# An attention kernel's VectorE exponentials: three shifted bit patterns with 64-bit adds on GpSimd, and PSUM banks and SBUF slots in shared pools

## Chip, core and metric

The kernel runs on one core of a Trainium2 chip. TensorE multiplies matrices into PSUM, ScalarE computes functions, VectorE does elementwise work, GpSimd works on SBUF, SyncE issues DMAs. The engines run at the same time (ScalarE, VectorE and TensorE are busy for 98, 94 and 92% of the same span in the kernel before), each in the fixed order that the program gives it, and wait for each other (TensorE's matmuls for ScalarE 36.6 us there). The metric is the time of one execution in microseconds (us), median of several runs; smaller is better.

## The reference, cut to what matters

There are two attention blocks of the same size, joined at the end. Block A is linear attention and is small. Block B is full softmax attention with 32 heads of width 16 over 2048 positions, and it makes nearly all the work:

```python
q, k, v = qkv[0], qkv[1], qkv[2]          # each [1, 32, 2048, 16]
scores = jnp.einsum("bhqd,bhkd->bhqk", q, k) * Dh ** -0.5
p = _softmax(scores, axis=-1)
o = jnp.einsum("bhqk,bhkd->bhqd", p, v)
```

The scores hold 32 x 2048 x 2048 numbers. In tiles of 128 partitions by 512 columns ("blocks") that is 2048 blocks of exponentials. A runtime test decides whether the plain exponential without subtracting the maximum is safe; with these inputs it always is, so the general path behind it never runs.

## The kernel before: the parts that the change touches

The source lays the instructions out in advance: a small scheduler written in Python assumes a duration for each operation, decides what goes to which engine in which order, and emits the fixed program. Each of the 2048 blocks goes through a score matmul (QK) into a PSUM bank, an exponential on ScalarE *or* on VectorE, and a weighted-sum matmul (PV) that accumulates into one PSUM bank. A unit is 64 blocks that share one PV bank. A round is four PV matmuls. Where TensorE would have nothing to do, the scheduler puts in filler matmuls with zero weights (`ZW`), which add nothing to the result.

ScalarE takes three or two banks at once (`ABL`), with two fixed slots. VectorE has two banks of its own, `DB`, which it shares with the projections and block A:

```python
    ABL = (3, 2)
    ...
        SCR = [ps("pS%d" % i, [128, ABL[i] * 512], F32) for i in range(2)]
        PVb = ps("pPV", [128, 512], F32)
        DB = ps("pD", [128, 1024], F32)
    ...
                    sch.add("act", lambda e: e.activation(PT[:, row, c0:c0 + w], SCR[sl][:, 0:w], ACTF.Exp, scale=SC),
                            reads=skeys(sl), writes=[("PT", row, sl)])
```

On VectorE the kernel builds the exponential out of other operations. It scales and shifts the score, writes it as a 16-bit integer and reads those bits as float16 (the exponent field then holds the integer part of the power of two). Three more VectorE operations split and correct the pattern, and two matmuls per block add the two parts:

```python
                    sch.add("dve", lambda e: e.tensor_scalar(DI[:, buf, i * 512:(i + n) * 512], DB[:, b0 * 512:(b0 + n) * 512],
                                                             ESC, EB, op0=ALU.mult, op1=ALU.add), ...
            ops = [
                (0.06 + w * 0.00026, lambda e: e.tensor_scalar(Q, I, 0x3FF, 0x3800, op0=ALU.bitwise_and, op1=ALU.bitwise_or), ik, qk_),
                (0.08 + w * 0.00052, lambda e: e.tensor_tensor(Qh, Ih, Qh, op=ALU.mult), ik + qk_, qk_),
                (0.06 + w * 0.00026, lambda e: e.tensor_scalar(I, I, 0xFC00, 8, op0=ALU.bitwise_and, op1=ALU.bitwise_or), ik, ik)]
```

GpSimd only sets up constants. The first of them, an identity matrix, is needed at once: TensorE transposes the first pieces of x with it.

```python
        def mk_ident(t, key):
            sch.add("pool", lambda e: e.memset(t[:], 0.0), writes=[key])
            sch.add("pool", lambda e: e.affine_select(out=t[:], in_=t[:], compare_op=ALU.not_equal, fill=1.0,
                                                     base=0, pattern=[[-1, 128]], channel_multiplier=1),
                   reads=[key], writes=[key])
```

## Time and profile before

| before | value | where it is read |
|---|---|---|
| time | 760.04 us | median of 3 runs, 759.95 to 761.25 |
| span in the profile | 758.5 us | the page's head; 1.6 us of the time lie outside it |
| ScalarE / VectorE / TensorE / GpSimd busy | 98 / 94 / 92 / 1% | part 1 |
| first exponential starts | 8.59 us | timeline of ScalarE |
| blocks on ScalarE / VectorE | 1592 / 456 | counts of the groups |

Parts 1 and 4 of the page of the kernel before: busy us, share of the span and number of instructions by engine; then the chain of waits that ended last, by engine.

```profile
PE 695.9 (92%) x6229; PEld 234.4 (31%) x6229; DVE 716.1 (94%) x1235; ACT 739.8 (98%) x675; POOL 8.5 (1%) x27
...
ACT 94%; PE 4%; DVE 1%; DMA 1%; SPq 0%; issue 0%; ACTq 0%
```

ScalarE (ACT) is busy nearly all the time and carries 94% of the chain, so only a change that shortens ScalarE's own work, or its idle time, can shorten the kernel. VectorE (DVE) is nearly full too, which matters for what can be moved to it.

The groups of the page: source line, engine, operation, output<-input, shapes, count | busy us, mean ns of one | idle us just before them and who ended most of it.

```profile
L869 ACT ACTIVATE PT<-pS 128x1536 f16<-128x1536 f32 x637 | 732.5, 1482 | 5.1 <-PE pD L712 2.8
L811 DVE TENSOR_SCALAR DI<-pD 128x512 int16<-128x512 f32 (+1 forms) x442 | 304.0, 698 | 18.1 <-PE pD L712 15.9
L925 DVE TENSOR_TENSOR DQ<-DI,DQ 128x1536 f16<-128x1536 f16 x153 | 144.1, 942 | 1.6
L924 DVE TENSOR_SCALAR DQ<-DI 128x1536 int16<-128x1536 int16 x153 | 83.7, 547 | 1.1
L926 DVE TENSOR_SCALAR DI<-DI 128x1536 int16<-128x1536 int16 x153 | 83.2, 544 | 0.7
```

The exponentials wait only 5.1 us in all. The last three lines are the chain behind VectorE's conversions: 311 us, as much as the conversions themselves.

The mean of 1482 ns for an exponential can't be used as its cost, since the records of neighbours overlap: 637 times 1482 ns would be 944 us, in a span of 758.5. The longest pieces of the chain of waits give the cost, because within one there is no idle time (start us, us, what):

```profile
342.91 61.02 ACT PT L869 x54
```

54 alternating three-bank and two-bank exponentials in 61.02 us make 2.26 us a pair. Where exponentials follow each other without a gap in this trace, their ends lie 1.343 us (three banks), 0.917 us (two) and 0.490 us (block A's, one bank) apart, in the median. The differences of these are 0.426 and 0.427 us per 512 columns, which leaves 0.063 us for each instruction, and 1.343 and 0.917 make the 2.26 of a pair; I call this the cost law. For the 318, 319 and 32 smaller ones of block A (0.49 us each) it gives 735.1 us (to within 0.2, by rounding); ScalarE's busy time without its 3.7 us of other work is 736.1.

### The profile page before, as it was taken

What the parts mean: (1) busy time and instruction counts of PE and PEld (TensorE: products, weight loads), DVE (VectorE), ACT (ScalarE), POOL (GpSimd) and SP (SyncE); (2) the same over time, 40 slices, a digit from 0 to 9 for tenths busy, and PEclk for the clock granted to TensorE, in tenths of its full rate; (3) what the DMA queues carried; (4) which work ended last, traced back from release to release, by engine and by line L of the source; (5) the groups of instructions that cost most, each with busy time, mean ns of one, the idle gap of its engine ahead of it and who ended that gap; (6) DMA issues with size and microseconds to landing.
All of it is one profiled execution on the core that took longest, in us unless ns stands there. A gap on an engine that the chain in (4) does not pass through costs nothing.

```text
span 758.5 us, 14741 instructions
## 1 busy us (share of the span) xinstructions
PE 695.9 (92%) x6229; PEld 234.4 (31%) x6229; DVE 716.1 (94%) x1235; ACT 739.8 (98%) x675; POOL 8.5 (1%) x27
## 2 busy tenths in 40 slices
PE   8999999999999899999989899999899889999996
PEld 4333232333333323223222332222242232323232
DVE  6899999899999989989999999989999999999994
ACT  6999999999999999999999999999999999999995
POOL 4000000000000000000000000000000000000000
PEclk9999999999999989999999999999999999999999
DMA  9900000000000000000000000000002001110001
GB/s 197 247 2 1 1 1 9 10 12 1 1 2 1 1 1 2 14 9 15 22 22 1 1 22 22 22 9 15 15 2 42 1 2 50 29 35 8 15 15 32
DMA packets 36568, 17.27 MB, mean 23 GB/s; under 512 B 27536, under 2 KB 35984, under 8 KB 36496
## 3 DMA queue, kind: packets, MB, share of 16 engines
q1 hardware_dynamic: 35408, 15.61, 8.6%
q8 instruction: 51, 0.84, 0.5%
q10 hardware_dynamic: 1088, 0.66, 0.3%
q14 instruction: 21, 0.17, 0.1%
HBM read 4.46 MB, written 4.19 MB: 11 GB/s over the span
## 4 chain that ended last, share of the span: by engine, by line
ACT 94%; PE 4%; DVE 1%; DMA 1%; SPq 0%; issue 0%; ACTq 0%
ACT PT L869 91%; ACT EA L571 2%; PE pPV L996 1%; PE pS L712 1%; DMA Wb<-in_B_wqkv_dram 1%; PE pS L1048 0%; PE pD L462 0%; DVE DI L811 0%; DVE DQ L925 0%; SPq L333 0%; ACT KNa L444 0%; DVE KNa L444 0%; PE pPV L1209 0%; PE pS L1090 0%; PE pD L661 0%
## 5 line engine op out<-in xcount | busy, mean ns | idle before, releaser
L869 ACT ACTIVATE PT<-pS 128x1536 f16<-128x1536 f32 x637 | 732.5, 1482 | 5.1 <-PE pD L712 2.8
L811 DVE TENSOR_SCALAR DI<-pD 128x512 int16<-128x512 f32 (+1 forms) x442 | 304.0, 698 | 18.1 <-PE pD L712 15.9
L712 PE MATMUL pS<-QT,KM 32*128 32x512 bf16 x1592 | 248.4, 386 | 50.0 <-ACT PT L869 36.6
L996 PE MATMUL pPV<-PT,VV 128*17 128x512 f16 x1592 | 204.7, 384 | 1.2 <-DVE OT L1023 1.2
L712 PE MATMUL pD<-QT,KM 32*128 32x512 bf16 x456 | 169.2, 386 | 0.8 <-issue 0.5
L925 DVE TENSOR_TENSOR DQ<-DI,DQ 128x1536 f16<-128x1536 f16 x153 | 144.1, 942 | 1.6
L712 PEld LDWEIGHTS pS<-QT,KM 32*128 32x128 bf16 x1592 | 60.8, 91 | 273.1 <-ACT PT L869 262.1
L996 PE MATMUL pPV<-DQ,VV 128*17 128x512 f16 x456 | 102.7, 386 | 1.0 <-DVE OT L1023 0.8
L996 PE MATMUL pPV<-DI,VV 128*17 128x512 f16 x456 | 101.7, 383 | 0.0
L1209 PE MATMUL pPV<-xTb,ZW 128*17 128x256 bf16 x593 | 93.9, 274 | 0.0
L924 DVE TENSOR_SCALAR DQ<-DI 128x1536 int16<-128x1536 int16 x153 | 83.7, 547 | 1.1
L926 DVE TENSOR_SCALAR DI<-DI 128x1536 int16<-128x1536 int16 x153 | 83.2, 544 | 0.7
L996 PEld LDWEIGHTS pPV<-PT,VV 128*17 128x17 bf16 x1592 | 43.9, 88 | 73.2 <-issue 63.1
L1209 PEld LDWEIGHTS pPV<-xTb,ZW 128*17 128x17 bf16 x593 | 45.2, 91 | 39.4 <-issue 29.4
L712 PEld LDWEIGHTS pD<-QT,KM 32*128 32x128 bf16 x456 | 40.1, 91 | 14.6 <-DVE DI L811 6.9
L580 PE MATMUL pD<-Wa,xTa 128*128 128x256 bf16 x256 | 39.0, 277 | 0.0
L462 PE MATMUL pD<-xTb,Wb 128*128 128x512 bf16 x120 | 34.7, 383 | 1.0 <-DVE DI L811 0.6
L996 PEld LDWEIGHTS pPV<-DQ,VV 128*17 128x17 bf16 x456 | 23.0, 88 | 24.7 <-issue 16.8
L996 PEld LDWEIGHTS pPV<-DI,VV 128*17 128x17 bf16 x456 | 26.5, 90 | 9.6 <-DVE DI L926 1.0
L571 ACT ACTIVATE EA<-pD 128x512 bf16<-128x512 f32 x32 | 27.3, 854 | 0.0
L1023 DVE STREAM_TRANSPOSE OT<-pPV 128x512 f32<-128x512 f32 x32 | 22.6, 708 | 4.4 <-PE pPV L996 4.4
L580 PEld LDWEIGHTS pD<-Wa,xTa 128*128 128x128 bf16 x256 | 20.2, 98 | 16.8 <-issue 9.0
(92 smaller groups left out, 327.6 us busy)
## 6 DMA issues: line engine op xcount, KB each, us to landing
out_dram<-KNa SPq DMA_DIRECT2D x30, 128.0 KB, 1.7
Wa<-in_A_wqkv_dram SPq DMA_DIRECT2D x1, 1536.0 KB, 7.3
KM<-KR SPq DMA_DIRECT2D x96, 16.0 KB, 1.8
Wb<-in_B_wqkv_dram SPq DMA_DIRECT2D x2, 384.0 KB, 5.7
Wb<-in_B_wqkv_dram SPq DMA_DIRECT2D x1, 512.0 KB, 4.8
WOb<-in_B_wo_dram SPq DMA_DIRECT2D x1, 512.0 KB, 8.2
WOa<-in_A_wo_dram SPq DMA_DIRECT2D x1, 512.0 KB, 9.0
ON<-in_B_x_dram ACTq DMA_DIRECT2D x1, 256.0 KB, 2.9
```

The source lines that it names most:

```text
L462: return e.matmul(f32v(bk), lhsT=Wb[:, cc, kind * 512 + Gp * 128:kind * 512 + Gp * 128 + 128], rhs=xTb[:, cc, sc * 512:(sc + 1) * 512], st ...
L571: ("act", 0.06 + n * 0.000833, f_ev("act", lambda e, bk: e.activation(EA[:, q, 0:n], f32v(bk)[:, c0:c0 + n], ACTF.Exp), [], [("EA", q)])),
L580: return e.matmul(f32v(bk)[:, 256 * tt:256 * tt + 256], lhsT=xTa[:, cc, (t2 + tt) * 128:(t2 + tt + 1) * 128], rhs=Wa[:, cc, 512 * kind + 2 ...
L712: return e.matmul(dst, lhsT=KM[32 * g:32 * g + 32, Gp % 2, e_, j * 128:(j + 1) * 128], rhs=QT[32 * g:32 * g + 32, Gp % 2, c * 512:(c + 1) ...
L811: sch.add("dve", lambda e: e.tensor_scalar(DI[:, buf, i * 512:(i + n) * 512], DB[:, b0 * 512:(b0 + n) * 512], ESC, EB, op0=ALU.mult, op1=A ...
L869: sch.add("act", lambda e: e.activation(PT[:, row, c0:c0 + w], SCR[sl][:, 0:w], ACTF.Exp, scale=SC), reads=skeys(sl), writes=[("PT", row, ...
L924: (0.06 + w * 0.00026, lambda e: e.tensor_scalar(Q, I, 0x3FF, 0x3800, op0=ALU.bitwise_and, op1=ALU.bitwise_or), ik, qk_),
L925: (0.08 + w * 0.00052, lambda e: e.tensor_tensor(Qh, Ih, Qh, op=ALU.mult), ik + qk_, qk_),
L926: (0.06 + w * 0.00026, lambda e: e.tensor_scalar(I, I, 0xFC00, 8, op0=ALU.bitwise_and, op1=ALU.bitwise_or), ik, ik)]
L996: sch.add("pe", lambda e, g=g, j=j, h=h, P=P, first=first, last_=last_: e.matmul(PVb[32 * g:32 * g + 17, 0:512], lhsT=VV[:, j, vcol(h):vco ...
L1023: sch.add("dve", lambda e: e.transpose(OT[:, 0, :], PVb[:, 0:512]), reads=[("PV", g) for g in range(4)], writes=[("OT", 0)])
L1209: ins = e.matmul(dst, lhsT=ZW[:, 0:17], rhs=xTb[:, 0, 0:256], start=first, stop=first, tile_position=(0, 32 * g))
```

## The change

Intent: let VectorE make more of the exponentials, so that ScalarE makes fewer. The chain of three operations goes. Instead the pattern is used three times, shifted by a third and two thirds of an octave, each with its own weight; the three errors are meant to cancel in part. The shift is an integer add on the bit pattern, which GpSimd does for four 16-bit patterns at a time in a 64-bit add. The weights are folded into copies of V, so the sum costs three PV matmuls per block instead of two. All seven PSUM banks besides PV's become one pool: ScalarE takes a third bank when it is free. All blocks in SBUF become one pool of 46 slots. The core of the diff (cut):

```diff
-    EB = 14754.203187
+    EB = 13680.651890
+    SHIFT = (0, 342, 683)
+    WGT = (1.0, 0.79296875, 0.62890625)
...
-        PT = sb("PT", [128, NPT, 5 * 512], F16)
-        DI = sb("DI", [128, NDG, DG * 512], I16)
-        DQ = sb("DQ", [128, NDG, DG * 512], I16)
+        PT = sb("PT", [128, NB * 512], F16)
+        PTi, PTl = PT.bitcast(I16), PT.bitcast(I64)
...
+        BANK = [(PS, PSb, i * 512, ("B", i)) for i in range(7)]
+        SLOT = ((0, 1), (4, 5))
+        OPT = (2, 3)
+        DSET = (6, 3, 2)
...
+            for k in (1, 2):
+                st.append(("dve", 0.2, f_op("dve", lambda e, k=k: e.tensor_scalar(
+                    VV[:, r, k, 4 * t4:4 * t4 + 4, :], VV[:, r, 0, 4 * t4:4 * t4 + 4, :], WGT[k], None, op0=ALU.mult), ...
...
-                        sch.add("dve", fn, reads=rd, writes=wr)          # the chain of three
+                c_ = SHIFT[k_]
+                v_ = c_ | c_ << 16 | c_ << 32 | c_ << 48
+                sch.add("pool", lambda e: e.int64_add(PTl[:, pos * 128:pos * 128 + w], PTl[:, p0 * 128:p0 * 128 + w], v_), ...
...
+                more = bfree[ob] is not None and bfree[ob] <= st and pt_room(3, st + 0.5) is not None
...
+                bl = grow(3 if more and ok(3) else 2)
```

Several settings of the scheduler change with it (`DG`, `PVQ`, `DBL`, `TEND` and others).

## The prediction

> **What bounds the kernel now.** ScalarE. The page's busy table has ScalarE 739.8 us of 758.5 (98%), and the chain of waits is 94% ScalarE, 91% of it the exponentials. VectorE is close behind (716.1 us, 94%). TensorE's 695.9 us (92%) flatter it: 629 filler matmuls are in it, and by the waits it stood 36.6 us on ScalarE's buffers. In the groups, the exponentials wait only 5.1 us in all.
>
> ScalarE's cost law, read from the timeline: an alternating 3-bank and 2-bank exponential takes 2.26 us a pair (54 of them in 61.02 us). With 0.427 us per 512 columns that leaves 0.063 us per instruction; a run of seven 3-bank and six 2-bank ones takes 14.90 us and fits.[...]
>
> **What the change removes, adds, moves** (counts from the built programs' order of instructions):
> - Exponentials: 2048 blocks of 128x512 in both. ScalarE's share falls from 1592 to 1521 blocks, VectorE's rises from 456 to 527. ScalarE instructions: 318 three-bank + 319 two-bank become 216 + 436 (+1 single). By the law, 719.5 us becomes 690.2; the 32 other exponentials stay. So -29.3 us on the critical path.
> - VectorE: the three-step chain behind each conversion (144.1 + 83.7 + 83.2 = 311 us) disappears. Conversions go from 304 to 479 x 0.682 + 24 x 1.211 = 356 us; scaling V adds 32 short operations (some 0.3 us each, from a similar one at 288 ns). Total about 470 us, 64%: VectorE stops being a second limit.
> - GpSimd: 517 + 20 64-bit adds. No trace shows their duration. From 524 ns for a 128x512 two-byte memset I estimate 0.5 to 0.9 us for a two-block add, 260 to 480 us in all: not a limit unless one takes over 1.3 us.[...]
> - TensorE: the second matmul of each VectorE block becomes three: 2504 weighted-sum matmuls become 3102. With 0.215 us per round of four and about 0.1 us at each change of kind (timeline), work without fillers rises from about 550 to about 588 us, 80% of the new span. Fillers fall from 629 to 208.
>
> **On the critical path:** only ScalarE's 29 us. VectorE's 245 us saved shorten nothing themselves; they allow the 71 blocks to move. Against it: two-bank exponentials are now two of three, so TensorE must refill in 0.92 us more often, and in its fixed order it also waits for GpSimd. I allow 4 us of extra ScalarE idle time. The first 8.6 us and last 10 us stay.
>
> **Prediction:** 760 - 29 + 3 = 734 us, 8 in 10 between 722 and 752. Faster by over 2%: 0.83; within 2%: 0.13; slower: 0.04.
>
> **What would show it:** ScalarE still 96 to 98% busy, about 711 us, with the exponentials' group near 703 us and idle under 12 us; VectorE 60 to 67%; GpSimd 35 to 65%; the chain still over 90% ScalarE.
>
> **What would make it wrong:** a 64-bit add far longer than estimated, so that TensorE waits for GpSimd and ScalarE starves (idle before exponentials, released by TensorE);[...] the first add's start-up; or a schedule laid out for durations the chip doesn't keep, so that short two-bank exponentials leave gaps.

Three passages are cut, marked where they stood. None of them was a term of the sum: it came to 760 - 29 + 3 = 734 us, and all its terms stand. The 0.427 and 0.063 us of the cost law are those measured above; for the 0.215 us of a round and the 0.1 us of a change of kind, single matmuls in the trace of the kernel before give 0.221 and 0.10 in the median.

## The result, and the profile after

The changed kernel took **741.11 us** (median of 4, 740.94 to 741.70) against 760.08 (median of 4). The ratio is 0.975, 95% interval 0.9737 to 0.9764: faster by 2.5%, inside the stated range but 7 us above its centre. Here and below a ratio is the mean time of one kernel's fast runs over that of the other's of the same rounds, so it is not quite the ratio of the quoted medians. All outputs are right.

Parts 1 and 4 of the page of the kernel after, the same lines as before:

```profile
PE 676.5 (91%) x6483; PEld 226.9 (31%) x6534; DVE 516.2 (70%) x865; ACT 711.2 (96%) x691; POOL 327.2 (44%) x562
...
ACT 88%; PE 8%; issue 2%; DVE 1%; ACTq 0%; POOL 0%; POOLq 0%
```

ScalarE still bounds the kernel, with 28.6 us less work; VectorE fell from 94 to 70%, GpSimd rose to 44%. ScalarE's part of the chain fell below 90%, though: something else got in. The groups that answer to those of before:

```profile
L903 ACT ACTIVATE PT<-pS 128x1024 f16<-128x1024 f32 (+1 forms) x653 | 702.4, 1332 | 9.6 <-PE pS L709 9.4
L977 POOL INT64_ADD PT<-PT x537 | 319.8, 608 | 385.2 <-DVE PT L805 339.0
L805 DVE TENSOR_SCALAR PT<-pS 128x512 int16<-128x512 f32 (+1 forms) x503 | 339.5, 708 | 88.4 <-PE pS L709 84.0
```

The adds take 0.61 us each, as estimated, and GpSimd idles more than half of the time. The exponentials' waits rose from 5.1 to 9.6 us. The largest change is at the very start. The timelines of ScalarE in the first microseconds (start us, us, engine line op, forms, count, [idle before <- who ended it]), first of the kernel before:

```profile
5.09 0.60 ACT L444 ACTIVATE xTb<-pS 128x512 bf16<-128x512 bf16 x1 [1.78 <-PE pS L1079]
7.16 0.38 ACT L1100 ACTIVATE QT<-pS 128x256 bf16<-128x256 f32 x1 [1.48 <-PE pS L1090]
8.59 13.67 ACT L869 ACTIVATE PT<-pS 128x1536 f16<-128x1536 f32 x12 [1.05 <-PE pS L712]
```

and of the kernel after:

```profile
10.72 0.60 ACT L454 ACTIVATE xTb<-pS 128x512 bf16<-128x512 bf16 x1 [7.44 <-PE pS L1109]
12.00 0.38 ACT L1130 ACTIVATE QT<-pS 128x256 bf16<-128x256 f32 x1 [0.68 <-PE pS L1120]
14.69 16.97 ACT L903 ACTIVATE PT<-pS 128x1536 f16<-128x1536 f32 x17 [2.30 <-PE pS L709]
```

The first exponential starts 6.1 us later. ScalarE waits there for TensorE's transposes (line 1109), and those wait for GpSimd. The wait of TensorE in the kernel after (who waited, for what: us in total, times, longest; the view names the GpSimd instruction that ended just before TensorE started, which follows the affine select of the identity):

```profile
PE pS L1109 <- POOL ZMk L385: 5.2, 1, 5.2
```

GpSimd's timeline of before:

```profile
1.24 0.29 POOL L358 TENSOR_SCALAR_AFFINE_SELECT identb<-identb 128x128 bf16<-128x128 bf16 x1 [0.23 <-POOL identb L357]
```

and of after, with its first add:

```profile
9.31 0.28 POOL L368 TENSOR_SCALAR_AFFINE_SELECT identb<-identb 128x128 bf16<-128x128 bf16 x1 [8.32 <-issue]
...
23.11 6.21 POOL L977 INT64_ADD PT<-PT  x11 [6.39 <-issue]
```

The affine select is the same instruction in both, ahead of every add; "issue" means that the profile shows nothing it waited for. In the view of these two source lines, an instruction `MODIFY_POOL_CONFIG` (two records of 11 ns) stands before the first affine select, at 1.2 us, and before the first add, at 16.8 us (duration ns min/median/max, first and last start us):

```profile
L368 POOLq MODIFY_POOL_CONFIG  x2: 11/11/11, 1.2 to 1.2; - x2
...
L977 POOLq MODIFY_POOL_CONFIG  x2: 11/11/11, 16.8 to 16.8; - x2
```

After them GpSimd has no record until 9.31 and 23.11 us. The kernel before has such a pair too, also at 1.2 us, but its affine select starts at once, at 1.24 us:

```profile
L358 POOLq MODIFY_POOL_CONFIG  x2: 11/11/11, 1.2 to 1.2; - x2
```

So the difference of the two spans, -19.1 us, splits like this:

| part | before | after | difference |
|---|---|---|---|
| start of the first exponential | 8.59 | 14.69 | +6.1 |
| ScalarE's busy time after that (without 3.7 us of other work) | 736.1 | 707.5 | -28.6 |
| waits before later exponentials | 4.05 | 7.3 | +3.2 |
| from the last exponential's end to the end | 9.76 | 9.87 | +0.1 |
| sum | 758.5 | 739.4 | -19.1 |

(The parts are rounded one by one. 5.1 and 9.6 us of the groups hold the waits of the very first exponentials, 1.05 and 2.30 us; the table takes those off.)

### The profile page after: what moved, and what is told of

Read it like the earlier page. It is cut to its first block, busy times and chain, and to the rows that moved or that the text cites. A ratio compares the mean times of both kernels' runs of the same rounds, so it can differ in the third digit from the quotient of the medians.

```text
span 739.4 us, 15721 instructions
## 1 busy us (share of the span) xinstructions
PE 676.5 (91%) x6483; PEld 226.9 (31%) x6534; DVE 516.2 (70%) x865; ACT 711.2 (96%) x691; POOL 327.2 (44%) x562
## 4 chain that ended last, share of the span: by engine, by line
ACT 88%; PE 8%; issue 2%; DVE 1%; ACTq 0%; POOL 0%; POOLq 0%
ACT PT L903 86%; PE pS L709 3%; PE pPV L1031 2%; ACT EA L569 2%; PE pS L657 1%; PE pS L472 1%; PE pS L1120 0%; PE pS L1078 0%; DVE PT L805 0%; PE pPV L1237 0%; PE pS L1237 0%; ACT KNa L454 0%; PE pS L547 0%; PE pS L1109 0%; DVE KM L486 0%
## 5 line engine op out<-in xcount | busy, mean ns | idle before, releaser
L903 ACT ACTIVATE PT<-pS 128x1024 f16<-128x1024 f32 (+1 forms) x653 | 702.4, 1332 | 9.6 <-PE pS L709 9.4
L977 POOL INT64_ADD PT<-PT x537 | 319.8, 608 | 385.2 <-DVE PT L805 339.0
L805 DVE TENSOR_SCALAR PT<-pS 128x512 int16<-128x512 f32 (+1 forms) x503 | 339.5, 708 | 88.4 <-PE pS L709 84.0
L709 PE MATMUL pS<-QT,KM 32*128 32x512 bf16 x2048 | 281.8, 386 | 37.9 <-ACT PT L903 27.6
L1031 PE MATMUL pPV<-PT,VV 128*17 128x512 f16 x3102 | 269.8, 383 | 0.5 <-DVE OT L1051 0.4
L578 PE MATMUL pS<-Wa,xTa 128*128 128x256 bf16 x256 | 38.7, 275 | 0.8 <-DVE PT L805 0.5
L472 PE MATMUL pS<-xTb,Wb 128*128 128x512 bf16 x98 | 29.8, 383 | 5.2 <-issue 2.1
L1237 PE MATMUL pPV<-xTb,ZW 128*17 128x256 bf16 x180 | 31.7, 274 | 0.0
L569 ACT ACTIVATE EA<-pS 128x512 bf16<-128x512 f32 x32 | 26.1, 815 | 0.0
L1237 PEld LDWEIGHTS pPV<-xTb,ZW 128*17 128x17 bf16 x180 | 14.4, 91 | 15.0 <-issue 10.2
```

The source lines that it names most:

```text
L472: return e.matmul(f32v(bk), lhsT=Wb[:, cc, kind * 512 + Gp * 128:kind * 512 + Gp * 128 + 128], rhs=xTb[:, cc, sc * 512:(sc + 1) * 512], st ...
L569: ("act", 0.06 + n * 0.000833, f_ev("act", lambda e, bk: e.activation(EA[:, q, 0:n], f32v(bk)[:, c0:c0 + n], ACTF.Exp), [], [("EA", q)])),
L578: return e.matmul(f32v(bk)[:, 256 * tt:256 * tt + 256], lhsT=xTa[:, cc, (t2 + tt) * 128:(t2 + tt + 1) * 128], rhs=Wa[:, cc, 512 * kind + 2 ...
L709: return e.matmul(dst, lhsT=KM[32 * g:32 * g + 32, Gp % 2, e_, j * 128:(j + 1) * 128], rhs=QT[32 * g:32 * g + 32, Gp % 2, c * 512:(c + 1) ...
L805: sch.add("dve", lambda e: e.tensor_scalar(PTi[:, i * 512:(i + n) * 512], PS[:, b0 * 512:(b0 + n) * 512], ESC, EB, op0=ALU.mult, op1=ALU.add),
L903: sch.add("act", lambda e: e.activation(PT[:, p0 * 512:p0 * 512 + w], PS[:, use[0] * 512:use[0] * 512 + w], ACTF.Exp, scale=SC), reads=[(" ...
```

## The experiments

Theory 1, *the share*: ScalarE is the limit, and the 71 blocks that moved to VectorE are all of the gain. Theory 2, *the start*: it is the 64-bit add's place among GpSimd's instructions, behind the affine selects, that makes the first affine select late (8.3 us) and then the first add (6.4 us). Theory 3, *the waits*: the +3.2 us come from the layout, either from VectorE durations assumed too short or from long PV batches. The rivals stand in the expectations.

All later runs but those marked use the early add of the first experiment. In the table, "later waits" are ScalarE's waits before exponentials after the first one. Each ratio is to the kernel before in the same rounds. Its median there was 760.08 us beside the changed kernel, 761.05 for a1 to d1, 761.36 for e1 to h1 and 761.0 for i1 to o1, on different chips, so a difference of about 1 us between times of different rounds means nothing:

| run | time us | ratio to before | blocks on ScalarE | cost law us | first exponential | later waits us |
|---|---|---|---|---|---|---|
| before | 760.08 | | 1592 | 735.1 | 8.59 | 4.1 |
| after | 741.11 | 0.975 | 1521 | 705.9 | 14.69 | 7.3 |
| a1_add_first | 735.84 | 0.967 | 1521 | 705.9 | 8.78 | 7.7 |
| b1_before_add (before + add) | 765.79 | 1.005 | 1592 | 735.1 | 14.03 | 4.1 |
| c1_share_as_before (no early add) | 762.44 | 1.001 | 1596 | 735.9 | 14.45 | 0.8 |
| d1_adds_on_dve (no add at all) | 746.87 | 0.981 | 1565 | 724.7 | 8.46 | 1.4 |
| e1_durations | 736.78 | 0.968 | 1535 | 712.3 | 8.40 | 3.2 |
| f1_fixed_banks | 742.77 | 0.975 | 1551 | 716.7 | 8.60 | 2.8 |
| g1_two_banks | 751.47 | 0.987 | 1527 | 715.5 | 8.41 | 11.6 |
| h1_relaid | 700.85 | 0.920 | 1451 | 677.0 | 10.22 | 1.8 |
| i1_short_batches | 728.35 | 0.958 | 1518 | 705.1 | 8.28 | 2.2 |
| m1_double_adds | 774.02 | 1.017 | 1570 | 727.5 | 8.68 | 18.8 |
| n1_before_relaid (of before) | 760.18 | 1.000 | 1590 | 734.2 | 8.48 | 3.6 |
| o1_dnext | 720.86 | 0.948 | 1496 | 695.0 | 8.40 | 3.4 |

### The start: an early add, and an add in the kernel before

```diff
+        sch.add("pool", lambda e: e.memset(PT[:, 0:8], 0.0), writes=[("PT", 0)])
+        sch.add("pool", lambda e: e.int64_add(PTl[:, 0:2], PTl[:, 0:2], 0), reads=[("PT", 0)], writes=[("PT", 0)])
         mk_ident(identb, "identb")
```

> The changed kernel with a two-element 64-bit add put in front of the first affine select on GpSimd[...]. Theory[...]: the 8.3 us that GpSimd's first affine select waited fall away, the first exponential starts near 8.6 us instead of 14.7, and the time falls by 5.5 to 7 us to about 735. Rival (the late start has another cause, such as the order of GpSimd's set-up or the larger program): the affine select still waits about 8 us and the time stays within 1 us of 741. Second rival (the early start is given back, because what follows was late for other reasons): start at 8.6 us but time above 738.

Measured: 735.84 us, 5.3 us less than the changed kernel (6 us by the ratios, 0.967 and 0.975). A `MODIFY_POOL_CONFIG` pair now stands in front of the early add. The view of the early add's line, and GpSimd's timeline, a1_add_first:

```profile
L373 POOLq MODIFY_POOL_CONFIG  x2: 11/11/11, 0.9 to 1.0; - x2
...
1.53 0.29 POOL L368 TENSOR_SCALAR_AFFINE_SELECT identb<-identb 128x128 bf16<-128x128 bf16 x1 [0.16 <-POOL identb L367]
```

Both "issue" waits, of 8.3 and 6.4 us, are gone, and the first exponential starts at 8.78 us. Between the two profiled executions the span falls by 6.0 us: 5.9 from the earlier start and 0.6 after the last exponential, less 0.4 of later waits and 0.2 of busy time.

The reverse, in the kernel before, with the add *last* in GpSimd's set-up and its result unused:

```diff
         sch.add("pool", lambda e: e.memset(VNa[:, :, :, 128:129], 1.0), writes=["VNa1"])
+        XA = sb("XA", [128, 8], F16)
+        XAl = XA.bitcast(I64)
+        sch.add("pool", lambda e: e.memset(XA[:], 0.0), writes=["XA"])
+        sch.add("pool", lambda e: e.int64_add(XAl[:, 0:2], XAl[:, 0:2], 0), reads=["XA"], writes=["XA"])
```

> The kernel before with one two-element 64-bit add at the end of GpSimd's set-up, its result unused. Theory[...]: [...] first affine select waits about 8 us, the first exponential starts near 14.7 us instead of 8.6, and the time rises by 5.5 to 7 us to about 766. Rival: the start is that of the kernel before and the time stays within 1 us of 760.

Measured: 765.79 us, 4.7 us above the kernel before in the same rounds (ratio 1.005, 95% interval 1.003 to 1.008). That is a little less than the 5.5 to 7 expected; the first exponential starts at 14.03 us, 5.4 later. GpSimd's waits in b1_before_add (who waited, for what: us in total, times, longest):

```profile
POOL identb L359 <- issue: 7.9, 1, 7.9
POOL XA L397 <- issue: 7.0, 1, 7.0
```

One tiny add costs 7.9 us in an instruction that stands *ahead* of it: the affine select that started after 0.23 us in the kernel before. The add hasn't run yet in that execution, so its own work there can't be the cause. In front of the affine selects, as in a1_add_first, an add brings no such wait: the first affine select starts after 0.16 us. That an add behind the affine selects makes the start late (first exponential 5.4 us later in b1_before_add), and that one in front of them takes this away (5.9 us earlier in a1_add_first), is shown. What fills the 8 us is not: in the kernel after GpSimd has no record between 1.25 and 9.31 us, and no run separates a first execution from a later one.

### The share: VectorE held to its old number of blocks

```diff
+        dn, DCAP = [0], 456 / 2048
...
+            if dn[0] > DCAP * (UB * NU - sum(left)):
+                return None
```

> The changed kernel with VectorE's share of the blocks capped at that of the kernel before: 1596 blocks on ScalarE (352 three-bank and 270 two-bank exponentials). Theory (only the moved blocks pay): 720 + 16 us of exponentials by the cost law, 14.7 us start, 9.9 us end, 4 to 8 us of gaps, so about 767 us, slower than both kernels, although VectorE is then below 67% busy. Rival (freeing VectorE or sharing the banks pays by itself): below 752.

Measured: 762.44 us, the time of the kernel before, with VectorE at 63% and GpSimd at 37%. Its later waits were 0.8 us, less than the 4 to 8 that I expected, which is why it came in below 767. With the old share, emptying VectorE and pooling the banks bring no more than the 3.3 us of waits, and the late start (5.9 us) more than cancels them in the profile.

### Who does the adds

In the changed kernel, without the early add:

```diff
-                sch.add("pool", lambda e: e.int64_add(PTl[:, pos * 128:pos * 128 + w], PTl[:, p0 * 128:p0 * 128 + w], v_),
+                sch.add("dve", lambda e: e.tensor_scalar(PTi[:, pos * 512:pos * 512 + 4 * w], PTi[:, p0 * 512:p0 * 512 + 4 * w], c_, None, op0=ALU.add),
...
-            push("pool", at, 1, POV + POW * n, r)
+            push("dve", at, 1, 0.1 + n * 0.133, r)
```

> The changed kernel with all 64-bit adds replaced by 16-bit adds on VectorE, laid out anew by the kernel's own scheduler: 1564 blocks on ScalarE, VectorE about 710 us busy. Theory (GpSimd's part is to let VectorE take more blocks):[...] start at 8.6 us, exponentials 724 us by the cost law, so about 750 us, 742 to 758; VectorE 93 to 97% busy. Rival (the adds could as well stay on VectorE): 738 or less.

Measured: 746.87 us. Part 1 of its page:

```profile
PE 677.6 (91%) x6466; PEld 227.9 (31%) x6513; DVE 634.3 (85%) x1316; ACT 729.0 (98%) x692; POOL 7.4 (1%) x25
```

ScalarE did what was expected, but VectorE is 85% busy, not 93 to 97%: I had added up records that overlap (in this trace the groups of VectorE add up to 691 us, for 634.3 us busy). By the ratios, 14 of the gain of 19 us come with VectorE's own 16-bit adds. Moving the adds to GpSimd is worth 44 more blocks and 11.0 us (against a1_add_first: the cost law falls by 18.8 us, but the later waits grow by 6.3), and half of that is lost again in the changed kernel by the late start.

The run shows a second thing. The groups of VectorE in the kernel before, in d1_adds_on_dve and in the kernel after, the division (two SBUF inputs) and the clamp of block A's exponential (16-bit, SBUF to SBUF); first before:

```profile
L1029 DVE TENSOR_TENSOR OT<-OT,ZR 128x256 bf16<-128x256 f32 x32 | 13.3, 414 | 0.1
L572 DVE TENSOR_SCALAR EA<-EA 128x512 bf16<-128x512 bf16 x32 | 9.2, 288 | 0.4
```

d1_adds_on_dve, without work for GpSimd:

```profile
L1059 DVE TENSOR_TENSOR OT<-OT,ZR 128x256 bf16<-128x256 f32 x32 | 13.3, 417 | 0.2
L570 DVE TENSOR_SCALAR EA<-EA 128x512 bf16<-128x512 bf16 x32 | 9.3, 290 | 8.8 <-ACT EA L569 8.4
L556 DVE TENSOR_SCALAR VV<-VV 128x544 bf16<-128x544 bf16 x32 | 8.3, 296 | 0.1
```

the kernel after:

```profile
L1059 DVE TENSOR_TENSOR OT<-OT,ZR 128x256 bf16<-128x256 f32 x32 | 16.6, 520 | 0.6
L556 DVE TENSOR_SCALAR VV<-VV 128x544 bf16<-128x544 bf16 x32 | 13.0, 440 | 0.3
L570 DVE TENSOR_SCALAR EA<-EA 128x512 bf16<-128x512 bf16 x32 | 11.7, 365 | 22.5 <-ACT EA L569 22.4
```

Beside GpSimd's adds these become 25 to 49% longer, while the conversions of one block out of PSUM keep their 682 ns (before and after; 684 in d1_adds_on_dve). The trace of the kernel after shows it by single instructions too: the divisions, scalings of V and clamps that no add overlaps (15, 12 and 11 of 32) take 420, 296 and 292 ns in the mean, those that lie almost wholly (over 95%) within adds (8, 11 and 11) 607, 581 and 480; conversions of one block take 681 and 684. What in the chip holds them up is not shown. It costs VectorE some 10 us in all and is off the critical path.

### The waits: assumed durations, and batch length

```diff
-                st.append(("dve", 0.2,  ... VV scaling
+                st.append(("dve", 0.42, ...
-        ("dve", 0.35, ... division
+        ("dve", 0.46, ...
-        ("dve", 0.08 + n * 0.00026, ... clamp
+        ("dve", 0.18 + n * 0.00026, ...
```

> The changed kernel with the early add, and with three of the scheduler's assumed VectorE durations set to those measured beside GpSimd's adds (scaling V 0.42 us instead of 0.20, the division 0.46 instead of 0.35, the small exponential's clamp 0.31 instead of 0.21). Theory (the 7.5 us of waits before exponentials come from a layout that trusts shorter VectorE times): the waits after the first exponential fall from 7.5 us to under 4; the layout now gives ScalarE 1535 blocks instead of 1521, so 712 us of exponentials, and the time is 734 to 737 us all the same. Rival (TensorE's long batches cause the waits): they stay at 6 to 9 us and the time is 739 to 743.

(The records' means for scaling V, the division and the clamp are 0.41, 0.52 and 0.37 us in a1_add_first and 0.44, 0.52 and 0.37 in the kernel after, so the settings are near what was measured, not equal to it.)

Measured: 736.78 us, later waits 3.2 us instead of 7.7. Waits and time are as theory 3's first form expected. Time didn't improve, because the new layout gave ScalarE 14 more blocks.

```diff
-    PVR = 3
+    PVR = 2
```

> The early add, and at most two rounds of weighted sums (8 matmuls) in one batch on TensorE instead of three; the assumed durations stay as they were. ScalarE's work is the same: 705 us by the cost law. Theory (the layout trusts VectorE times that are too short, and that makes the waits): waits after the first exponential stay at 5 to 8 us, time 734 to 738. Rival (long batches that a two-bank exponential can't cover make the waits): they fall under 3 us and the time to 729 to 732.

Measured: 728.35 us with later waits of 2.2 us: the rival's numbers, though the assumed durations were left as they were. So either edit removes most of the waits. So do layouts with neither edit: c1_share_as_before has 0.8 us and d1_adds_on_dve 1.4. A three-round PV batch takes 0.75 us (the next QK starts that long after it in the timeline), and with the 0.32 us of a QK this overfills the 0.92 us that a two-bank exponential covers. The gap of 1.02 us at 569 us in the changed kernel shows the batches at work (timeline of all engines, cut):

```profile
566.95 0.70 DVE L1051 STREAM_TRANSPOSE OT<-pPV 128x512 f32<-128x512 f32 x1
...
567.11 1.03 PE L657 MATMUL pS<-WOa,KNa 128*128 128x512 bf16 x4
...
568.07 0.83 PE L1031 MATMUL pPV<-PT,VV 128*17 128x512 f16 x12
568.83 0.61 PE L709 MATMUL pS<-QT,KM 32*128 32x512 bf16 x7
...
569.26 1.02 ACT L903 ACTIVATE PT<-pS 128x1024 f16<-128x1024 f32 x1 [1.02 <-PE pS L709]
```

Block A's matmuls and then twelve PV matmuls stand ahead of ScalarE's scores. VectorE isn't late here: its transpose, which frees the PV bank, ends at 567.65, while TensorE is still on block A's four matmuls, and PV starts 0.31 us after the last of them has started, much as the QK starts 0.32 us after the last round of PV (times of single instructions in the trace). How much each of the two causes holds by itself is not settled: every edit lays the whole program out anew. In time, the short batches bring 7.5 us against a1_add_first, the measured durations nothing.

### Banks, and the width of an exponential

The banks split as in the kernel before (three and two for ScalarE, two for the rest):

```diff
-        OPT = (2, 3)
-        DSET = (6, 3, 2)
+        OPT = (2, None)
+        DSET = (6, 3)
...
-                more = bfree[ob] is not None and ...
+                more = ob is not None and bfree[ob] is not None and ...
-                if more and d_backlog(st) < DLOW:
+                if more and d_backlog(st) < -1.0:
```

> The early add, and the PSUM banks split as in the kernel before: three banks and two for ScalarE's two slots, two for VectorE and the projections. The scheduler then gives ScalarE 1551 blocks (308 three-bank, 313 two-bank). Theory (sharing the banks is what lets VectorE take some 30 more blocks; nothing else): exponentials 716 us by the cost law, 8.8 us start, 9.9 end, 1.6 outside the span, 2 to 7 us of waits, so 738 to 744 us against 736 of the run with the early add. Rival (bank sharing is the larger part of the gain): above 750.

Measured: 742.77 us, as expected. Sharing the banks is worth 30 blocks, 6.9 us against a1_add_first.

Every exponential two banks wide:

```diff
-                more = bfree[ob] is not None and ...
+                more = False and bfree[ob] is not None and ...
```

> The early add, and every exponential two banks wide (763 instead of 653 instructions for 1526 blocks). Theory (each exponential costs 0.063 us besides its columns, and a third bank where one is free is worth that): exponentials 715 us by the cost law instead of 705, so 742 to 748 us against 736 of the run with the early add. Rival (instruction count doesn't matter where they run back to back): 734 to 738.

Measured: 751.47 us, above the expected range of 742 to 748. The cost law's 9.6 us over a1_add_first are in it: about 7 us for 111 more instructions and 2.6 us for 6 more blocks. Of the rest, 3.9 us are later waits. By the profiles another 1.7 are busy time above the law, for the most part, by my estimate, because an exponential that starts after a wait has a record of 1.02 us (the one after the gap above; 10 such two-bank ones in the kernel after have a median of 1.02) where one in a row costs 0.917, and 1.1 lie after the last exponential. Part 1 of its page, and the waits of its exponentials:

```profile
PE 705.4 (94%) x6468; PEld 225.4 (30%) x6468; DVE 505.8 (67%) x834; ACT 722.7 (96%) x802; POOL 324.0 (43%) x560
...
ACT PT L905 <- PE pS L711: 12.2, 23, 1.6
```

23 waits instead of 12. Each exponential has its own small cost (0.063 us), and a narrow one leaves TensorE less time for the refill (0.917 us, not 1.343).

### Was the change used to the full?

The scheduler decides how many blocks VectorE gets, so I drew 400 random sets of its settings with the early add and the measured durations, and took a layout with few blocks on ScalarE. The draw itself needs no chip; what this one is worth, the chip says (settings of several lines put into one):

```diff
-    DNEXT, PVR, PVQ, JB = 20, 3, 12.5, 1
+    DNEXT, PVR, PVQ, JB = 4, 2, 10.0, 2
-    ALAG, TEND, PVO, DLOW, DLEAD = 30.0, 640.0, 16, 1.0, 0.5
+    ALAG, TEND, PVO, DLOW, DLEAD = 60.0, 660.0, 14, 1.5, 0.4
```

> The early add, the measured durations, and eleven of the scheduler's settings chosen anew, so that it hands VectorE 597 blocks instead of 527 and never puts more than two rounds of weighted sums in one batch. ScalarE: 1451 blocks, 118 three-bank and 548 two-bank exponentials, 676 us by the cost law. Theory (the moved blocks are all that pays, and the new VectorE path had room for twice as many): 8.8 + 676 + 9.9 + 1.6 and 5 to 10 us of waits, so 699 to 708 us, VectorE 75 to 82% busy, TensorE still not the limit. Rival (TensorE, with 3242 weighted-sum matmuls, becomes the limit): above 715, with ScalarE waiting over 20 us for TensorE.

Measured: **700.85 us**, 0.920 of the kernel before (95% interval 0.9174 to 0.9225), faster than both kernels. (Nine settings differ; `DEND` and `RES` were drawn too and came out as they were.) Part 1 of its page, and its exponentials:

```profile
PE 664.7 (95%) x6541; PEld 205.5 (29%) x6541; DVE 550.4 (79%) x919; ACT 681.4 (97%) x705; POOL 368.4 (53%) x626
...
L905 ACT ACTIVATE PT<-pS 128x1024 f16<-128x1024 f32 (+1 forms) x667 | 674.5, 1350 | 3.9 <-PE pS L711 3.7 <-PE pPV L1033 0.2
```

The VectorE path had room for 141 blocks more than before, not 71. ScalarE is still the limit: it waits 3.9 us. TensorE comes closer, with 15% of the chain that ended last against 8% in the kernel after.

One setting alone, on top of the measured durations:

```diff
-    DNEXT = 20
+    DNEXT = 4
```

> The run with the measured durations and one more setting: VectorE goes on taking blocks of the current unit until 4 are left instead of 20. ScalarE: 1496 blocks, 694.5 us by the cost law. Theory (moved blocks are all that pays): 8.8 + 694.5 + 9.9 + 1.6 and 3 to 7 us of waits, so 717 to 723 us against 737. Rival (blocks taken so late in a unit hold up its last weighted sums, and TensorE with it): above 728.

Measured: 720.86 us. Letting VectorE take blocks of the current unit until 4 are left, not 20, moves 39 blocks and brings 15.9 us against e1_durations.

The control, in the kernel before: the best of 300 draws of the same kind (`PVR = 2`, `DNEXT = 16`, `DEND = 16`, `PVQ = 11.0`, `PVO = 18`, `DLEAD = 0.6`, `JB = False`). Its built program has 1590 blocks on ScalarE, one fewer than the expectation says.

> The kernel before with the best of 300 random draws of its own scheduler's settings: 1591 blocks on ScalarE instead of 1592. Theory (in the kernel before VectorE was full, so no layout could move blocks; the room that the relaid kernel uses was made by the change): 757 to 761 us. Rival (relaying alone is what gains): below 750.

Measured: 760.18 us, the same as the kernel before. There VectorE is 95% busy, and no layout found could move blocks.

### How long may an add be?

```diff
+                for _ in range(2):
                     sch.add("pool", lambda e: e.int64_add(...), ...
-            push("pool", at, 1, POV + POW * n, r)
+            push("pool", at, 1, 2 * (POV + POW * n), r)
```

> The early add, and every 64-bit add done twice over (same result), the scheduler told so: GpSimd about 590 us busy. The scheduler gives ScalarE 1570 blocks instead of 1521, 727 us by the cost law. Theory (a slower add costs through the share of blocks that it lets VectorE take, well before GpSimd is full): 750 to 757 us, GpSimd 76 to 81% busy. Rival, and what the prediction said (an add is no limit until one takes over 1.3 us; here a pair takes 1.2): under 741.

Measured: 774.02 us, worse than all three numbers, the prediction's, the theory's and the time of the kernel before. Part 4 of its page, by engine, and four waits of ScalarE, TensorE, VectorE and GpSimd:

```profile
POOL 53%; ACT 34%; PE 5%; issue 5%; DVE 2%; DMA 1%; ACTq 0%; DVEq 0%; POOLq 0%
...
ACT PT L905 <- PE pS L711: 15.4, 34, 1.5
PE pPV L1034 <- POOL PT L980: 6.3, 19, 0.6
DVE PT L807 <- POOL PT L980: 38.8, 29, 3.9
POOL PT L980 <- DVE PT L807: 123.6, 18, 38.8
```

GpSimd is only 76% busy here, yet it leads the chain. Four pauses of 8.5 to 38.8 us make 107.8 us of its idle time; between them it works with gaps of about 0.1 us. There TensorE waits in its fixed order for the patterns, and ScalarE for TensorE; VectorE too waits for GpSimd, 38.8 us in all. The theory that the longer add costs only through the share (750 to 757) was too mild as well: 18.8 us of waits come on top of the share, and ScalarE is busy 7.8 us more than by the cost law (1.8 in a1_add_first).

## Why the prediction was right, and where it was off

1. *ScalarE bounds the kernel, and the moved blocks are the gain.* Right, and shown: c1_share_as_before takes the gain away, h1_relaid and o1_dnext enlarge it as the cost law says. Predicted -29.3 us of exponentials; ScalarE's busy time fell by 28.6. The profile is close to what was named in advance: 711.2 us busy (711), 702.4 in the exponentials' group (703), 9.6 idle (under 12). The prediction names the timeline for the 54 exponentials; they stand in the chain of waits.
2. *"The first 8.6 us and last 10 us stay."* This is the step that failed. The last part stayed (9.87 us); the first became 14.69. This term is +6.1 us of the 7 between 734 and 741. The result is inside the range because the range was wide, not because this was foreseen. The start-up of the first add was named as a risk, but I looked at the place of the add, where the wait of 6.4 us costs little, and not at GpSimd's first affine select, which waited 8.3 us.
3. *"I allow 4 us of extra ScalarE idle time"* (the sum took 3): measured +3.2 for the later waits. The size was right. Its stated cause, that TensorE must refill more often in 0.92 us, fits g1_two_banks and i1_short_batches. The other stated cause, TensorE waiting for GpSimd, hardly shows: 1.4 us in five waits of its weight loads for the adds.
4. *GpSimd.* 0.5 to 0.9 us an add was predicted, 0.61 measured; 35 to 65% busy, 44 measured. But "not a limit unless one takes over 1.3 us" was wrong: a pair of 1.2 us gave 774 us. I compared a sum with the span and forgot that TensorE takes the patterns in a fixed order, and that the adds come in bursts.
5. *VectorE at 60 to 67%, about 470 us.* Measured 70%, 516.2 us. The larger part is the sum: in the kernel before the groups of VectorE add up to 793 us for 716.1 busy, since records overlap. The prediction took the records of the conversions and the chain, 615 us, off the busy time, and so left 101 us for the rest, whose own records add up to 178. The longer operations from SBUF to SBUF, scaling V with 0.44 us instead of 0.3 among them, are only some 10 of the 46 us.
6. *"They allow the 71 blocks to move."* Right but too small in view: by h1_relaid there was room for 141, so that the changed kernel uses about half of what it makes possible.
7. *The chain over 90% ScalarE.* It was 88%: the late start and the waits are TensorE's and "issue" in it.

## What to carry to other kernels

When an engine is the limit, cost a change by how many units of its work move elsewhere, then ask who decides that number: here freeing VectorE paid only as far as the scheduler handed it blocks, and new settings doubled the number of blocks moved, from 71 to 141. If a new GpSimd operation joins others in a program, as the 64-bit add joined the affine selects here, try a tiny one of its kind in front of them: here that gave back about 6 us (the span fell from 739.4 to 733.4). So look at the first 15 us of the profile after adding any new GpSimd operation. An engine's busy share doesn't tell whether its results come in time where another engine reads them in a fixed order: in m1_double_adds GpSimd was 76% busy, led the chain and made the kernel 774.02 us.
